# Hash bits of an attention head in three matmul passes instead of four

## The chip, the cores and the metric

One core of one Trainium2 chip runs the program. The metric is device time in microseconds (us) from start to end of one execution; the median of the runs counts.

## The reference

LSH attention over 2 batches of 8 heads (768 positions, head size 64) is followed by two gated dense blocks. Of the attention, what matters here:

```python
q_bits = (np.einsum('bhsd,dk->bhsk', q, proj) > 0)      # proj: 64 x 6
k_bits = (np.einsum('bhsd,dk->bhsk', k, proj) > 0)
q_bucket = np.sum(q_bits * 2 ** np.arange(6), axis=-1)  # same for k
mask = q_bucket[:, :, :, None] == k_bucket[:, :, None, :]
scores = np.where(mask, scale * q @ k.T, -1e9)
out = softmax(scores) @ v
```

Two positions attend to each other only if the signs of all six projections agree. A wrong sign changes a whole row, so the projection has to be close to exact.

## The kernel before, in words

The program works through 16 heads. For each, `prep` (L378) brings q and k into the form of matmul operands, six tiles of 128 queries then run through scores, maximum, exponential, transposition and the product with v, and the weights of the dense blocks are decoded from 64-bit numbers in between. The dense blocks follow; part of the first one runs beside the later heads.

Numbers are carried as two parts that a matmul takes at full speed, a high part (the number rounded) and a low part (what is left). `split` (L360) makes them with q and k apart, as 64 + 64 columns of a tile `spq` or `spk`. In `prep`, six transposes of such a tile go to `psT` buffers, tiles of PSUM of which there are four for the whole stage (`psT`, L278), and ScalarE copies them into `aq` or `ak` (L390): rows 0 to 63 hold the high part, rows 64 to 127 the low part. SyncE copies rows into `bq` and `bk` (L393, L395), the operands of the second score matmul.

The hash follows at L398 to L405. For each half of 384 positions one PSUM tile `gps` collects the projections of q in one set of rows and of k in the other:

```python
for n, nm in enumerate(("aq", "ak")):
    for x in range(2):
        pe.matmul(ps[:, :HS], lhsT=pq[n][x], rhs=m[nm][:, hs], start=n + x == 0, stop=n + x == 2)
```

`pq[n][0]` is the high part of the projection, `pq[n][1]` the low part, each placed for both the high and the low rows of the operand. VectorE turns signs into numbers (`ft`, L402), and SyncE copies them into the lower halves of the score operands (L406, L407). These numbers make the score of a pair with differing bits too small to matter. So `gps` is computed with four matmuls for each half, eight for a head, 120 for heads 1 to 15. Head 0 has its own code, `first_head`, with eight more (L447).

The order of the work is a list schedule: `order_engines` (L40) gives each instruction a cost and each hand-over between engines a delay, walks through time by priorities, and fixes the order of the rows on every engine, SyncE's queue included. An instruction that isn't ready holds up all that stands behind it on its engine. `prep` for the next head is spread over the tiles of the head before.

Of the kernel before, what the change touches and what calls it, by code (L numbers as in the profile page):

```python
# [11 lines left out]
F32R = mybir.dt.float32r  # L12
# [216 lines left out]
def lsh_attention_moe_moe2_kernel(  # L229
# [21 lines left out]
    B, H, S, D = q.shape  # L251
    P = 128
    NB = proj.shape[1]
    NT = S // P
    HS = S // 2
# [14 lines left out]
    dve = nc.vector  # L270
    pool = nc.gpsimd
    pe = nc.tensor
    sync = nc.sync
# [4 lines left out]
    def f(ap):  # L278
        return ap.bitcast(F32)

    cst = Tiles(ctx.enter_context(tc.tile_pool(name="cst", bufs=1, side="left")), "cst", 1)
# [6 lines left out]
    idr = cst.tile([P, P], F32R, name="idr")  # L288
    pq_raw = cst.tile([P, NB], F32, name="pq_raw")
    pq = [[cst.tile([P, P], F32R, name=f"pq{a}{i}") for i in range(2)] for a in "qk"]  # L290
    thr = cst.tile([P, 2], F32, name="thr")
    lim = cst.tile([P, 2], F32, name="lim")

# [56 lines left out]
    def load_head(h, nms):  # L350
        if not 0 <= h < NH:
            return
        b, hh = divmod(h, H)
        for nm, src in (("q", q), ("k", k), ("v", v)):
            if nm in nms:
                t = ap_.tile([P, NT, D], F32, tag="raw" + nm, name=f"raw{nm}{h}", bufs=1)
                sync.dma_start(out=t, in_=src[b, hh].rearrange("(p c) d -> p c d", c=NT))
                raws[h, nm] = t

    def split(h, nm, part):  # L360
        if not 0 <= h < NH:
            return
        if part == 0:
            t = ap_.tile([P, NT, 2, D], F32R, tag="sp" + nm, name=f"sp{nm}{h}", bufs=2 if nm == "v" else 1)
            splits[h, nm] = t
            (pool if h >= 2 else dve).tensor_copy(t[:, :, 0, :], raws[h, nm])
        else:
            t = splits[h, nm]
            (dve if h < 2 and nm != "v" else pool).tensor_tensor(out=t[:, :, 1, :], in0=raws[h, nm], in1=f(t[:, :, 0, :]), op=ALU.subtract)

    def alloc_mats(h):
        m = {}
        for nm in ("aq", "bq", "ak", "bk"):
            m[nm] = ap_.tile([P, S], F32R, tag=nm, name=f"{nm}{h}")
        m["ft"] = ap_.tile([P, S], F32R, tag="ft", name=f"ft{h}", bufs=1)
        mats[h] = m

    def prep(h):  # L378

        load_head(h, "v")  # L380
        if h < NH:
            alloc_mats(h)
            m = mats[h]
            for nm, d in (("q", "aq"), ("k", "ak")):
                t = splits[h, nm]
                for half in range(2):
                    ps = psT.tile([P, 512], F32R, tag="t", name="trr")
                    for c in range(3):
                        pe.transpose(ps[:, c * P:(c + 1) * P], t[:, half * 3 + c].rearrange("p a d -> p (a d)"), idr)
                    act.activation(out=m[d][:, half * HS:(half + 1) * HS], in_=f(ps[:, :HS]), func=AF.Copy,  # L390
                                   scale=SCALE if nm == "q" else 1.0)
                    if nm == "q" and half == 1:
                        sync.dma_start(out=f(m["bq"][0:D]), in_=f(m["aq"][0:D]))  # L393
                    yield
            sync.dma_start(out=f(m["bk"][0:D]), in_=f(m["ak"][D:P]))  # L395
            for half in range(2):
                hs = slice(half * HS, (half + 1) * HS)
                ps = psT.tile([P, 512], F32, tag="t", name="gps")  # L398
                for n, nm in enumerate(("aq", "ak")):
                    for x in range(2):  # L400
                        pe.matmul(ps[:, :HS], lhsT=pq[n][x], rhs=m[nm][:, hs], start=n + x == 0, stop=n + x == 2)  # L401
                dve.tensor_scalar(out=m["ft"][:, hs], in0=ps[:, :HS], scalar1=thr[:, 0:1], scalar2=thr[:, 1:2],  # L402
                                  op0=ALU.is_gt, op1=ALU.mult)
                if half == 0:
                    yield  # L405
            sync.dma_start(out=f(m["bk"][D:P]), in_=f(m["ft"][0:D]))  # L406
            sync.dma_start(out=f(m["bq"][D:P]), in_=f(m["ft"][D:P]))  # L407
            sync.dma_start(out=f(m["ak"][D:P]), in_=f(m["ak"][0:D]))
            yield
        for nm in "qk":  # L410
            split(h + 1, nm, 0)
            split(h + 1, nm, 1)
        load_head(h + 2, "qk")
        split(h - 1, "v", 0)
        split(h - 1, "v", 1)
# [391 lines left out]
    for n, (r0, sg) in enumerate(((D, 1.0), (0, -1.0))):  # L807
        for x in range(2):
            dve.memset(f(pq[n][x]), 0.0)
        for b0, sgn in ((r0, sg), (r0 + o, -sg)):  # L810
            hi, lo = (t[:, b0:b0 + NB] for t in pq[n])
            dve.tensor_scalar(out=hi, in0=pq_raw, scalar1=sgn, scalar2=None, op0=ALU.mult)
            dve.scalar_tensor_tensor(out=lo, in0=pq_raw, scalar=sgn, in1=f(hi), op0=ALU.mult, op1=ALU.subtract)
    dve.memset(thr[D:P, 1:2], -BIG)
    dve.memset(thr[0:D, 1:2], 1.0)
    dve.memset(thr[:, 0:1], 0.0)
# [19 lines left out]
    for _ in prep(1):  # L836
        pass
    pgs = {}

    def emit_prep(s):  # L840
        if s + 2 >= NT:
            h, i = divmod(s + 2, NT)
            if i == 0:
                pgs[0] = prep(h + 1)
            prio(s, -300)
            for _ in range(PAT[i]):
                next(pgs[0], None)
            if i == NT - 1:
                for _ in pgs[0]:
                    pass  # L850
# [74 lines left out]
```

## Time and profile before

| what | us |
|---|---|
| median of 3 runs | 856.51 (855.91 to 858.85) |
| the profiled execution, its own time | 857.49 |
| its span, first to last instruction | 855.5 |
| PE busy (share of the span) | 805.7 (94%) |
| DVE busy | 592.3 (69%) |
| ACT busy | 525.2 (61%) |
| POOL busy | 283.5 (33%) |
| mean granted clock of TensorE, of full speed | 0.996 |

The page's shares are averages over stages. Up to about 387 us the heads run and PE and DVE are both busy nearly all the time; from some 570 us on only dense matmuls are left and DVE has little to do. Matmul records overlap in a pipeline, so their mean length (some 350 ns for 384 columns) is not the time that one more matmul costs; the pieces of the chain, which don't overlap, tell that. The line names `PE`, `PEld` (weight load), `DVE` (VectorE), `ACT` (ScalarE), `POOL` (GpSimd) and `SP` (SyncE, which issues all transfers) are those of the profile.

### The profile page before, as it was taken

Reading aid. Unit: us, or ns where it says so; the run is one execution under the profiler, and the core shown is the slowest. Engines: PE = TensorE matmul, PEld = TensorE weight load, DVE = VectorE, ACT = ScalarE, POOL = GpSimd, SP = SyncE. Lnnn points to the kernel's source line nnn. Section 1 sums busy time; section 2 is a strip of 40 time slices with the busy share of each in tenths; the row PEclk is TensorE's granted clock in tenths of the full one; section 3 lists DMA queues with packets and bytes.
Section 4 is the critical chain, followed back from the end, with each engine's and each line's share of the span. In section 5 each row is a group of like instructions: output and inputs, shape, how many; then the busy total and the mean of one; then the engine's idle time right before and its main releaser. Section 6 shows DMA issues by size and latency. Waiting matters only on the chain.

```text
span 855.5 us, 12210 instructions
## 1 busy us (share of the span) xinstructions
PE 805.7 (94%) x4272; PEld 681.2 (80%) x4272; DVE 592.3 (69%) x1059; ACT 525.2 (61%) x1024; POOL 283.5 (33%) x236
## 2 busy tenths in 40 slices
PE   4777999999979999999999999999999999999998
PEld 3656888889878889897788777778888888888886
DVE  5999999998889999999569999972222222222222
ACT  4778878887778988888347656663334433343331
POOL 1343323232325343227423342343333323333230
PEclk9999999999989999999999999999999999999999
DMA  7555555443334544323105433400000000010001
GB/s 223 150 172 173 147 135 128 123 105 99 84 110 104 161 112 124 81 59 109 49 10 172 162 124 128 144 1 1 1 0 26 26 1 0 1 50 1 0 1 49
DMA packets 44908, 71.54 MB, mean 84 GB/s; under 512 B 6128, under 2 KB 32752, under 8 KB 44848
## 3 DMA queue, kind: packets, MB, share of 16 engines
q1 hardware_dynamic: 44848, 70.78, 28.7%
q8 instruction: 33, 0.54, 0.3%
q14 instruction: 27, 0.22, 0.1%
HBM read 52.43 MB, written 3.19 MB: 65 GB/s over the span
## 4 chain that ended last, share of the span: by engine, by line
PE 56%; DVE 29%; ACT 7%; issue 5%; DMA 2%; SPq 0%; DVEq 0%; ACTq 0%
PE pa L698 12%; PE m L698 11%; PE pb L698 11%; DVE da L338 4%; DVE pt L524 4%; PE tp L520 3%; PE av L537 3%; DVE s L476 3%; PE p L698 3%; DVE da L336 3%; PE wacc L593 3%; PE s L466 2%; PE gps L401 2%; ACT e L487 2%; PE s L469 2%
## 5 line engine op out<-in xcount | busy, mean ns | idle before, releaser
L738 DVE TENSOR_TENSOR pb<-pb,a 128x512 f32<-128x512 f32 x52 | 36.1, 694 | 138.8 <-PE pb L698 134.8
L520 PE MATMUL tp<-idf,e 128*128 128x128 f32 x576 | 100.8, 275 | 3.0 <-DVE pt L524 1.5
L524 DVE TENSOR_TENSOR pt<-tp,pt 128x384 fp32r<-128x384 f32 x192 | 100.7, 547 | 3.4 <-ACT pt L523 2.2
L523 ACT ACTIVATE pt<-tp 128x384 fp32r<-128x384 f32 x192 | 89.8, 494 | 21.1 <-PE tp L520 19.9
L487 ACT ACTIVATE e<-s,sm 128x768 f32<-128x768 f32 x96 | 95.9, 1000 | 10.2 <-DVE sm L477 9.7
L698 PE MATMUL pa<-x,wah 128*128 128x512 f32 x320 | 99.9, 390 | 1.4 <-DVE x L681 1.4
L698 PE MATMUL pb<-x,wbh 128*128 128x512 f32 x320 | 98.7, 389 | 0.0
L692 POOL TENSOR_TENSOR wal<-xall,wah 128x512 fp32r<-128x512 f32 x36 | 48.3, 1341 | 148.8 <-ACT wah L276 132.1
L476 DVE TENSOR_REDUCE s<-s 128x1 f32<-128x768 f32 x96 | 91.5, 954 | 8.6 <-PE s L469 8.5
L520 PEld LDWEIGHTS tp<-idf,e 128*128 128x128 f32 x576 | 71.5, 141 | 15.2 <-DVE pt L524 3.0
L334 ACT ACTIVATE da<-st 128x512 f32<-128x512 f32 x76 | 51.2, 673 | 47.0 <-DVE w1r L343 21.5
L537 PE MATMUL av<-pt,spv 128*128 128x256 f32 x576 | 78.7, 287 | 0.6 <-DVE pt L524 0.5
L537 PEld LDWEIGHTS av<-pt,spv 128*128 128x128 f32 x576 | 72.1, 191 | 2.8 <-DVE pt L524 0.9
L466 PE MATMUL s<-ak,aq 128*128 128x384 f32 x192 | 63.1, 385 | 9.3 <-ACT e L487 7.3
L698 PEld LDWEIGHTS pa<-x,wah 128*128 128x128 f32 x320 | 60.1, 188 | 14.7 <-DVE x L681 2.2
L593 PE MATMUL wacc<-wo,t 128*128 128x512 f32 x192 | 68.5, 420 | 2.9 <-POOL wo L588 1.4
L698 PEld LDWEIGHTS pb<-x,wbh 128*128 128x128 f32 x320 | 60.1, 188 | 12.5
L338 DVE SCALAR_TENSOR_TENSOR da<-st,da 128x512 uint32<-128x512 uint32 x76 | 64.6, 850 | 0.4
L698 PE MATMUL pa<-x,wal 128*128 128x512 f32 x160 | 62.3, 389 | 0.0
L698 PE MATMUL pb<-x,wbl 128*128 128x512 f32 x160 | 62.2, 389 | 0.0
L469 PE MATMUL s<-bk,bq 128*128 128x384 f32 x192 | 57.6, 365 | 0.0
L276 ACT ACTIVATE wah<-xall 128x512 fp32r<-128x512 f32 x36 | 22.7, 631 | 56.6 <-PE pa L698 56.6
(159 smaller groups left out, 1910.2 us busy)
## 6 DMA issues: line engine op xcount, KB each, us to landing
st<-in_moe_w_dram SPq DMA_DIRECT2D x32, 512.0 KB, 3.9
st<-in_moe_w_out_dram SPq DMA_DIRECT2D x20, 512.0 KB, 3.3
st<-in_moe_w_gate_dram SPq DMA_DIRECT2D x12, 512.0 KB, 3.5
st<-in_moe_w_val_dram SPq DMA_DIRECT2D x12, 512.0 KB, 3.5
rawq<-in_q_dram SPq DMA_DIRECT2D x16, 192.0 KB, 2.5
rawk<-in_k_dram SPq DMA_DIRECT2D x16, 192.0 KB, 3.3
rawv<-in_v_dram SPq DMA_DIRECT2D x16, 192.0 KB, 2.4
bq<-aq SPq DMA_DIRECT2D x16, 192.0 KB, 2.6
```

Source lines behind the costliest of these rows:

```text
L334: act.activation(out=f(a), in_=f(hw), func=AF.Abs)
L338: dve.scalar_tensor_tensor(out=a, in0=hw, scalar=0xC0000000, in1=a, op0=ALU.bitwise_and, op1=ALU.bitwise_or)
L466: pe.matmul(s[:, half, :HS], lhsT=m["aq"][:, qs], rhs=m["ak"][:, ks], start=True, stop=False)
L469: pe.matmul(s[:, half, :HS], lhsT=m["bq"][:, qs], rhs=m["bk"][:, ks], start=False, stop=True)
L476: dve.tensor_reduce(out=one[:, 1:2], in_=s[:, :, :HS], op=ALU.max, axis=AX.XY, negate=True)
L487: act.activation(out=e.rearrange("p (a c) -> p a c", a=2), in_=s[:, :, :HS], func=AF.Exp, bias=sm[:, 1:2], scale=sm[:, 0:1], accum_out=su_ ...
L520: pe.transpose(ps[:, j * P:(j + 1) * P], e[:, c * P:(c + 1) * P], idf)
L523: act.activation(out=dh, in_=src, func=AF.Copy)
L524: dve.tensor_tensor(out=lo[:, g % 2, half * 3:half * 3 + 3], in0=src, in1=f(dh), op=ALU.subtract)
L537: pe.matmul(acc[:, :2 * P].rearrange("p (a t) -> p a t", a=2), lhsT=w, rhs=r[:, :, c], start=(c == 0 and i == 0), stop=(c == NT - 1 and i ...
L593: pe.matmul(acc, lhsT=t3[x][:, j], rhs=wo[y][:, j], start=(j == 0 and n == 0), stop=(j == NF1 - 1 and n == 2))
L698: mm = pe.matmul(ps, lhsT=lhs[x], rhs=rhs[y], start=start and n == 0, stop=stop and n == 2)
```

## The change

The low part of the projection is needed against the high rows of q and of k only. The change lays these two sets of rows above each other in one operand: rows 0 to 63 of `bq` hold the high rows of q already, and a new copy puts the high rows of k into rows 64 to 127, which are free until `ft` is written there. A new constant `pl` stacks the two low parts of the projection, and one matmul with it takes the place of two. The products of the low part with the low rows, which were included before, fall away.

```diff
--- before.py
+++ after.py
@@ -288,6 +288,7 @@
     idr = cst.tile([P, P], F32R, name="idr")
     pq_raw = cst.tile([P, NB], F32, name="pq_raw")
     pq = [[cst.tile([P, P], F32R, name=f"pq{a}{i}") for i in range(2)] for a in "qk"]
+    pl = cst.tile([P, P], F32R, name="pl")
     thr = cst.tile([P, 2], F32, name="thr")
     lim = cst.tile([P, 2], F32, name="lim")
 
@@ -392,13 +393,13 @@
                     if nm == "q" and half == 1:
                         sync.dma_start(out=f(m["bq"][0:D]), in_=f(m["aq"][0:D]))
                     yield
+            sync.dma_start(out=f(m["bq"][D:P]), in_=f(m["ak"][0:D]))
             sync.dma_start(out=f(m["bk"][0:D]), in_=f(m["ak"][D:P]))
             for half in range(2):
                 hs = slice(half * HS, (half + 1) * HS)
                 ps = psT.tile([P, 512], F32, tag="t", name="gps")
-                for n, nm in enumerate(("aq", "ak")):
-                    for x in range(2):
-                        pe.matmul(ps[:, :HS], lhsT=pq[n][x], rhs=m[nm][:, hs], start=n + x == 0, stop=n + x == 2)
+                for n, nm in enumerate(("aq", "ak", "bq")):
+                    pe.matmul(ps[:, :HS], lhsT=pq[n][0] if n < 2 else pl, rhs=m[nm][:, hs], start=n == 0, stop=n == 2)
                 dve.tensor_scalar(out=m["ft"][:, hs], in0=ps[:, :HS], scalar1=thr[:, 0:1], scalar2=thr[:, 1:2],
                                   op0=ALU.is_gt, op1=ALU.mult)
                 if half == 0:
@@ -811,6 +812,8 @@
             hi, lo = (t[:, b0:b0 + NB] for t in pq[n])
             dve.tensor_scalar(out=hi, in0=pq_raw, scalar1=sgn, scalar2=None, op0=ALU.mult)
             dve.scalar_tensor_tensor(out=lo, in0=pq_raw, scalar=sgn, in1=f(hi), op0=ALU.mult, op1=ALU.subtract)
+    for n in range(2):
+        (act_copy if n else dve.tensor_copy)(pl[n * D:(n + 1) * D], f(pq[n][1][n * D:(n + 1) * D]))
     dve.memset(thr[D:P, 1:2], -BIG)
     dve.memset(thr[0:D, 1:2], 1.0)
     dve.memset(thr[:, 0:1], 0.0)
```

The new order was built with the same planner, and the rows of all engines moved. Three places are shown. First PE at the hash of head 11, `gps` with the preceding row, before (names end in the number of a tile, `aq_3212` and `ak_3214` are head 11's; line numbers are those of the file in question, one higher here after the change):

```order
L698 MATMUL p_3180<-xh,wl 128x512
L401 MATMUL gps<-aq_3212,pqq_72 128x384
L401 MATMUL gps<-aq_3212,pqq_73 128x384
L401 MATMUL gps<-ak_3214,pqk_74 128x384
L401 MATMUL gps<-ak_3214,pqk_75 128x384
L401 MATMUL gps<-aq_3212,pqq_72 128x384
L401 MATMUL gps<-aq_3212,pqq_73 128x384
L401 MATMUL gps<-ak_3214,pqk_74 128x384
L401 MATMUL gps<-ak_3214,pqk_75 128x384
L466 MATMUL s_83<-ak_2903,aq_2901 128x384 x2
L469 MATMUL s_83<-bk_2904,bq_2902 128x384 x2
```

and after the change, where `aq_3205`, `ak_3207` and `bq_3206` are head 11's:

```order
L521 MATMUL tp_3305<-idf,e_3183 128x128 x3
L402 MATMUL gps<-aq_3205,pqq_72 128x384
L402 MATMUL gps<-ak_3207,pqk_74 128x384
L402 MATMUL gps<-aq_3205,pqq_72 128x384
L402 MATMUL gps<-ak_3207,pqk_74 128x384
L699 MATMUL p_3334<-xh,wh 128x512
L521 MATMUL tp_3346<-idf,e_3224 128x128 x2
L402 MATMUL gps<-bq_3206,pl 128x384 x2
L467 MATMUL s_84<-ak_2897,aq_2895 128x384 x2
```

Two matmuls are gone, and the third pass of both halves stands behind the first two passes of both halves and three more matmuls, one of a dense layer (`p`) and two transposes (`tp`).

Second, PE at the hash of head 6, after the change, from right behind the second pass of the second half to the third passes:

```order
L467 MATMUL s_84<-ak_1370,aq_1368 128x384
L594 MATMUL wacc_1575<-wo_93,t_3_1499 128x512
L467 MATMUL s_84<-ak_1370,aq_1368 128x384
L594 MATMUL wacc_1575<-wo_92,t_3_1500 128x512
L470 MATMUL s_84<-bk_1371,bq_1369 128x384
L594 MATMUL wacc_1575<-wo_92,t_3_1499 128x512
L470 MATMUL s_84<-bk_1371,bq_1369 128x384
L594 MATMUL wacc_1575<-wo_93,t_3_1499 128x512
L594 MATMUL wacc_1575<-wo_92,t_3_1500 128x512
L578 MATMUL w3t_1808<-idf,w3f 128x128
L467 MATMUL s_85<-ak_1370,aq_1368 128x384
L402 MATMUL gps<-bq_1675,pl 128x384 x2
```

More rows of other work (`s` scores, `wacc` a product of weights, `w3t` its transposes) stand between the passes here than in head 11. Before, the four passes of each half were one block in this head too.

Third, SP's queue at the preparation of head 11, before:

```order
L393 DMA bq_3213<-aq_3212 64x768
L357 DMA rawq_3472<-in_q_dram 128x384
L395 DMA bk_3215<-ak_3214 64x768
L501 DMA row_3236<-rs_3233 128x6
L357 DMA rawk_3474<-in_k_dram 128x384
L408 DMA ak_3214<-ak_3214 64x768
L406 DMA bk_3215<-ft_3216 64x768
L407 DMA bq_3213<-ft_3216 64x768
```

and after the change:

```order
L394 DMA bq_3206<-aq_3205 64x768
L358 DMA rawq_3464<-in_q_dram 128x384
L502 DMA row_3229<-rs_3226 128x6
L396 DMA bq_3206<-ak_3207 64x768
L397 DMA bk_3208<-ak_3207 64x768
L506 DMA rr_2922<-row_3229 64x768
L358 DMA rawk_3466<-in_k_dram 128x384
L409 DMA ak_3207<-ak_3207 64x768
L319 DMA st<-in_moe_w_dram 128x4x128
L407 DMA bk_3208<-ft_3209 64x768
L408 DMA bq_3206<-ft_3209 64x768
```

The new copy `bq_3206<-ak_3207` comes right before the copy into `bk`, and the later copies are one row further back; the row copies (`row`, `rr`) moved as well.

## Rows read from the trace of the kernel before

**Rows 1.** Busy time of each engine by stage, whole run; columns in the first row.
```profile
core 0: us, PE busy (x) PEld busy (x) DVE busy (x) ACT busy (x) POOL busy (x), PEclk, DMA share, GB/s
0.00:20.00 20.00, 8.10 (x34) 7.25 (x35) 10.89 (x40) 9.04 (x17) 1.91 (x8) 1.00 0.79 229
20.00:387.00 367.00, 339.92 (x2232) 299.36 (x2231) 342.41 (x675) 297.25 (x626) 121.87 (x116) 0.99 0.45 122
387.00:570.00 183.00, 175.96 (x771) 142.02 (x770) 164.98 (x240) 112.85 (x204) 74.47 (x47) 1.00 0.32 104
570.00:855.50 285.50, 281.70 (x1242) 232.59 (x1240) 74.05 (x108) 106.09 (x180) 85.23 (x66) 1.00 0.03 12
```

**Rows 2.** The same view, the first 40 us of the heads.
```profile
20.00:60.00 40.00, 30.95 (x183) 24.96 (x181) 37.82 (x73) 30.17 (x62) 16.62 (x16) 1.00 0.55 159
```

**Rows 3.** Chain of waits from 20 to 387 us, shares by engine, tile and line.
```profile
by line: DVE pt L524 8.4%; PE tp L520 8.1%; PE av L537 7.6%; DVE s L476 7.0%; PE wacc L593 6.4%; PE s L466 5.3%; PE gps L401 5.2%; ACT e L487 5.0%; PE s L469 4.7%; issue 4.4%; PE p L698 3.9%; DVE da L338 3.1%; ACT pt L523 2.9%; DVE da L336 
```

**Rows 4.** Pieces of the chain: start us, length us, what, how many instructions.
```profile
221.99 0.47 PE wacc L593 x2
...
320.63 1.42 PE av L537 x12
...
322.79 0.35 PE s L469 x2
...
326.30 1.39 PE gps L401 x8
...
330.75 0.33 PE tp L520 x3
```

**Rows 5.** Timeline of head 15's preparation: start us, length us, engine, line, what.
```profile
343.16 0.46 PE L389 MATMUL trr<-idr,spk 128*128 128x128 f32 x3
...
344.63 0.47 SPq L395 DMA_DIRECT2D bk<-ak  x1
...
346.22 0.51 PE L401 MATMUL gps<-aq,pqq 128*128 128x384 f32 x2
...
347.31 0.67 DVE L402 TENSOR_SCALAR ft<-gps,thr 128x384 fp32r<-128x384 f32 x1
```

**Rows 6.** Instructions of line 408, which copies `ak[0:64]` up: min/median/max.
```profile
L408 SPq DMA_DIRECT2D ak<-ak x15: 461/467/549, 26.0 to 348.1; - x15
...
DMA to landing us min/median/max: 2.5/2.6/6.0
```

**Rows 7.** The same view for line 395, the copy into `bk` (ns, then us).
```profile
L395 SPq DMA_DIRECT2D bk<-ak x15: 461/467/468, 21.8 to 344.6; - x15
...
DMA to landing us min/median/max: 2.6/3.7/6.9
```

**Rows 8.** The start: timeline of DVE, then the chain's piece of the copy.
```profile
4.92 0.55 DVE L369 TENSOR_TENSOR spk<-rawk,spk 128x384 fp32r<-128x384 f32 x1
...
5.39 0.15 DVE L813 SCALAR_TENSOR_TENSOR pqk<-pq_raw,pqk 128x6 fp32r<-128x6 f32 x1
...
7.64 9.88 DMA ak<-ft
```

**Rows 9.** Waits of PE: who waited for whom, us in total, times, longest.
```profile
PE s L466 <- ACT e L487: 7.3, 5, 5.0
...
PE tp L520 <- DVE pt L524: 1.5, 2, 1.3
```

**Rows 10.** Busy time around 245 us (columns as in rows 1), and the chain's piece there.
```profile
240.00:245.00 5.00, 0.91 (x3) 0.91 (x4) 5.00 (x10) 3.11 (x6) 1.26 (x1) 0.72 0.38 131
245.00:250.00 5.00, 5.00 (x26) 4.87 (x25) 3.30 (x8) 1.87 (x5) 0.70 (x2) 0.59 0.08 28
...
246.59 2.56 PE av L537 x12
```

**Rows 11.** Costliest groups of the page: evictions of transposed halves, busy us, mean ns.
```profile
L524 DVE TENSOR_TENSOR pt<-tp,pt 128x384 fp32r<-128x384 f32 x192 | 100.7, 547 | 3.4 <-ACT pt L523 2.2
L523 ACT ACTIVATE pt<-tp 128x384 fp32r<-128x384 f32 x192 | 89.8, 494 | 21.1 <-PE tp L520 19.9
```

## Prediction

> **What bounds the kernel now.** I read the busy time by stage first [rows 1]: from 387 us on the program holds only dense layers, which the change does not touch. The reader should look at the stage from 20 to 387 us, where all 120 hash matmuls that change lie: PE is busy for 339.92 us of 367 and DVE for 342.41. Neither engine is far ahead of the other. PE's busy time is also generous, since matmul records overlap. At the spacing of back-to-back work on the chain [rows 4] (a transpose 0.33 / 3 = 0.11 us, a score matmul 0.35 / 2 = 0.175, one of `av` 1.42 / 12 = 0.118, a 512-column one 0.47 / 2 = 0.235, a hash matmul 1.39 / 8 = 0.174), the stage's 2,232 PE instructions need about 319 us. PE work therefore takes 367 / 319 = 1.15 of its bare length.
>
> The chain of waits, cut to this stage, goes back and forth between the two engines and gives `gps` 5.2% of it [rows 3], 19.1 us, of 120 x 0.174 = 20.9 us in all: nine tenths of the hash matmuls lie on the path that sets the end. Blocks of eight are unbroken PE work [rows 4].
>
> **The change, part by part.** *Removed:* one of four passes, two matmuls for each of 15 heads, so 30 x 0.174 = 5.22 us of PE. The bounds of the gain are 0, if DVE (342.41 of 367 us busy) simply becomes what is late, and 5.2, if all of it comes off the end. I take the chain's share, 0.91 x 5.22 = 4.8 us. It is nearest because the rows of the chain are those that set the end; DVE's work is not late next at most of these blocks, since the chain runs through PE there.
>
> *Added, a wait on the path:* the third pass reads `bq[64:128]`, which a new copy fills from `ak[0:64]`. Before, nothing stood between the copy of `ak` out of PSUM and `gps`. Now SP issues a transfer and PE waits for it if the rows in between don't cover it. In the head shown [rows 5] the transposes of k end at 343.62 (343.16 + 0.46) and SP issues at 344.63, 1.0 us later; I take 1.1 with the semaphore. The landing has two near rows. The copy of the same rows of `ak` to the same upper partitions took 2.6 us in the median [rows 6]. The copy issued where the new one now stands, right behind the loads, took 3.7, and 6.9 at the worst [rows 7]. So PE needs 3.7 us of other work from the end of the k transposes to the third pass, by the first row, and 4.8 by the second. I take 2.6, because source, size and target partitions are the same.
>
> What covers it is read from the new order at the spacings above, times 1.15: 2.2, 3.3, 4.6, 4.1, 6.1, 6.3, 5.6, 5.1, 4.1, 3.5, 2.9, 4.6, 4.0, 4.2 and 5.0 us for heads 1 to 15. At 3.7, heads 1, 2, 10 and 11 fall short, by 1.5, 0.4, 0.2 and 0.8. The first two lie before 60 us, where PE is busy only 30.95 of 40 us [rows 2], and I cost them at nothing; if that cover is gone they cost 1.9. That leaves 1.0 us; with some scatter of the landing I take 1.5. At 4.8 the shortfalls sum to 10.5, of which 6.4 lie behind head 2. The term's bounds are 0 and 10.5.
>
> *A rule on such copies.* The Trainium skill (DMA: Bandwidth & Descriptors, section Anatomy of one DMA — SWDGE (gpsimd) path) fits a copy as about 2.0 us fixed plus its bytes at 436 GB/s, an estimate of 2.45 us for 196,608 bytes, wherever it stands; the trace's 3.7 and 6.9 [rows 7] disagree, and these copies are issued by SP, not by GpSimd. By that rule the waits behind head 2 would be about 0.8 us and the time 0.7 lower than my sum; by [rows 7] the time is the first rival's.
>
> *The queues.* Every head adds one issue on SP, 0.467 us [rows 7], ahead of `bk<-ak` and of whatever follows; 15 of them are 7 us over 330, and the pushed copies are wanted only when that head's scores begin, which in the new order stand 8 to 14 us of PE work (at the spacings above) behind its third pass. I cost it at nothing. The later write of `bq[64:128]` with `ft` must wait for the third pass, but `ft` is made from that pass, so this adds no new wait. DVE's `ft` moves behind the third pass; what is queued behind it on DVE are evictions and decode steps, and if PE is late there, DVE is late too: the second rival.
>
> *The start.* Two copies build `pl`. The new order puts DVE's copy and one small operation ahead of the second half of the split of k, on the chain that leads to the transposes and the 9.88 us copy [rows 8]. Its price lies between 0.15 us, that small operation, and 0.55 us, the split itself, which handles more [rows 8]; for the two of them I take 0.3 us.
>
> **Sum.** -4.8 + 1.5 + 0.3 = -3.0 us against the profiled execution's own 857.49 us, so 854.5. That execution stood 0.98 above the median of 856.51, so in medians 853.5. A measurement can tell about 0.3%, 2.6 us, from no change; 853.5 is just outside.
>
> **The rivals.**
> *The landing eats the gain.* The copy lands as [rows 7] do, since in most heads a load of weights or of q stands directly ahead of it on SP. Then 6.4 us of waits take the place of 1.5: 853.5 + 4.9 = 858.4 if all of it counts, 856 if half is covered by DVE work that PE would have waited for anyway. For it: same place in the queue. Against: the larger cover of heads 3 to 9.
>
> *Slower: the hash tiles hold two of the four `psT` buffers.* Before, a tile's first matmul and the start of its `ft` are 347.31 - 346.22 = 1.1 us apart [rows 5]. Now both tiles are opened by their first two passes and stay open until the copy has landed, 2 to 4 us in most heads, while transposes and `av` share the other two. A transposed half holds its buffer for 0.33 + 0.494 + 0.547 = 1.4 us [rows 4, 11]. If one such half per head waits for one eviction by DVE, 15 x 0.547 = 8.2 us come on top: 861.7. Against it: PE waited only 1.5 us for these evictions in the whole run [rows 9]. It decides for slower from 5.7 us of such waits on.
>
> *The clock falls.* PE's one wait of 5.0 us for `e` [rows 9] was followed by a granted clock of 0.72 and 0.59 of 2.4 GHz, on average between the two levels [rows 10], and an `av` group took 2.56 instead of 1.42 us. If a copy lands at 6.9, PE waits 1.1 + 6.9 - 3 = 5 us, and such a stop costs about 7: 860.5. The Trainium skill (TensorE: Matmul & The Clock Gate, section HAM oscillation — how this bites in real kernels) shows a kernel whose waits for transfers throttle every tile; by that, each late head would pay. The shorter waits that I expect are against it.
>
> *The old stall goes.* The order around 240 us changes too. If the 5.0 us wait and the slow clock behind it vanish, about 7 us more are saved: 846.5. The rows of DVE work that caused it stand there in nearly the same sequence, which speaks against it.
>
> **Chances.** Forecast 0.42 (its own range 851 to 855.5), landing rival 0.27 (855 to 859), buffers 0.18 (858 to 863), clock 0.05, stall gone 0.08. Of the forecast about 0.32 lies below 853.9, with the 0.08 this gives 0.40 for faster. Within 0.3% are the other 0.10 of the forecast and 0.22 of the landing rival, 0.32. Slower: 0.05 of the landing rival, 0.18 and 0.05, so 0.28. The range from 848 to 862 leaves out most of the vanished stall and the upper end of the buffers and the clock, under 0.2.
>
> **What would show it.** Right: 90 hash matmuls in place of 120 and the new copy landing at 2.5 to 3 us; PE's waits for DMA `bq<-ak` a few us in total, in heads 1, 2, 10 and 11; the stage of the heads shorter by about 3 us, the dense stage unchanged at 285 us. Wrong: landings near 3.7 with waits in most heads; waits of `tp` for `pt` well above 1.5 us; DVE waiting for `gps` for more than a few us; a second dip of the granted clock.

## The result, and the profile after

The changed kernel takes 867.57 us in the median (866.35 to 868.77, 4 runs) beside 857.00 for the kernel before (855.91 to 858.85, 4 runs): ratio 1.0118 (1.0103 to 1.0133), some 10 us slower where 3 us faster was forecast. Below, ratios are turned into time at 857.0 us. Their intervals are 1.0 to 2.4 us to either side, and a difference of two such times is uncertain by some 1.7 us. The profiled execution after took 868.77 us with a span of 867.0.

Busy time by stage after, the same events as borders (columns as in [rows 1]):

```profile
20.00:394.00 374.00, 341.39 (x2195) 296.76 (x2194) 340.69 (x677) 298.46 (x630) 124.21 (x117) 0.97 0.48 128
394.00:581.00 187.00, 178.47 (x774) 144.37 (x774) 161.99 (x237) 111.83 (x201) 73.94 (x47) 0.98 0.31 100
581.00:867.00 286.00, 282.11 (x1244) 232.92 (x1242) 74.46 (x108) 106.46 (x180) 85.28 (x66) 1.00 0.03 12
```

Against [rows 1] the heads are 7 us longer, the stage behind them 4, and the dense stage is the same. So there are two places to look at. PE's waits name both:

```profile
PE s L467 <- ACT e L488: 7.9, 5, 4.4
PE gps L402 <- DMA bq<-ak: 6.9, 6, 2.9
...
PE y L699 <- DVE gl L659: 5.0, 1, 5.0
...
PE tp L521 <- DVE pt L525: 1.7, 5, 0.5
```

`bq<-ak` is the new copy, and this wait is new. The view of the tile `bq` gives 12.2 us for it. That counts a matmul and the weight load in front of it apart, though they mostly stand idle at the same time; with the longer of the two at each stop it is 9.2 us in nine heads. The line of the copy, 396, gives its landing:

```profile
L402 PE MATMUL gps<-bq,pl x30: 331/338/448, 24.9 to 356.7; 128*128 128x384 f32 x30
...
  DMA bq<-ak: 12.2, 12
```

```profile
L396 SPq DMA_DIRECT2D bq<-ak x15: 467/467/1144, 21.4 to 352.6; - x15
...
DMA to landing us min/median/max: 2.7/3.4/7.2
```

The worst is head 5, in the timeline (start us, length us, engine, line, what, in brackets the wait ahead of it):

```profile
120.48 0.33 SPq L319 DMA_DIRECT2D st<-in_moe_w_dram  x1
...
120.90 0.47 SPq L396 DMA_DIRECT2D bq<-ak  x1
...
122.83 0.33 PE L402 MATMUL gps<-ak,pqk 128*128 128x384 f32 x1
...
128.27 0.59 PE L402 MATMUL gps<-bq,pl 128*128 128x384 f32 x2 [2.85 <-DMA bq<-ak]
...
128.72 1.26 DVE L403 TENSOR_SCALAR ft<-gps,thr 128x384 fp32r<-128x384 f32 x2 [2.58 <-PE gps L402]
```

A load of weights, `st`, of 512 KB was issued 0.42 us ahead on the same queue. In this kernel the landing of each copy follows how far ahead such a load stands:

| head | `st` issued ahead by, us | copy lands after, us |
|---|---|---|
| 5 | 0.42 | 7.2 |
| 6 | 0.48 | 5.8 |
| 7 | 0.71 | 5.4 |
| 3 | 1.04 | 3.9 |
| 12 | 1.16 | 4.3 |
| 14 | 1.57 | 3.2 |
| 2 | 1.87 | 2.7 |
| 4 | 2.65 | 2.7 |

In the other seven heads, with no `st` within 2.6 us ahead, it lands after 2.7 to 3.5 us.

The second place is the start of the dense work. There VectorE makes `gl`, the low part of an operand (`p` less its high part `gh`), and the dense matmul `y` reads it. PE waits 5.0 us for `gl`, idles from 415 us on, and then works at half clock, 1.2 GHz (windows of 5 us, columns as in [rows 1]):

```profile
415.00:420.00 5.00, 0.81 (x4) 0.35 (x2) 5.00 (x6) 0.41 (x1) 2.83 (x2) 1.00 0.35 105
420.00:425.00 5.00, 4.16 (x10) 3.29 (x11) 4.46 (x8) 0.34 (x1) 0.00 (x0) 0.50 0.36 108
425.00:430.00 5.00, 5.00 (x20) 4.05 (x19) 0.69 (x1) 1.68 (x4) 2.62 (x3) 0.82 0.00 0
```

### The profile page after: what moved, and what is told of

It is laid out like the page before. It is cut to its first block, busy times and chain, and to the rows that moved or that the text cites. A ratio compares the mean times of both kernels' runs of the same rounds, so it can differ in the third digit from the quotient of the medians.

```text
span 867.0 us, 12169 instructions
## 1 busy us (share of the span) xinstructions
PE 810.4 (93%) x4242; PEld 681.5 (79%) x4242; DVE 587.8 (68%) x1060; ACT 525.0 (61%) x1025; POOL 285.2 (33%) x236
## 4 chain that ended last, share of the span: by engine, by line
PE 57%; DVE 25%; ACT 6%; DMA 5%; issue 5%; POOL 1%; SPq 0%; DVEq 0%; ACTq 0%; POOLq 0%
PE pa L699 12%; PE m L699 11%; PE pb L699 11%; PE av L538 5%; PE tp L521 4%; DVE da L339 4%; DMA bq<-ak 4%; PE wacc L594 3%; DVE da L338 3%; DVE da L337 3%; PE p L699 3%; DVE s L477 3%; PE s L467 2%; DVE pt L525 2%; PE s L470 2%
## 5 line engine op out<-in xcount | busy, mean ns | idle before, releaser
L521 PE MATMUL tp<-idf,e 128*128 128x128 f32 x576 | 103.7, 279 | 3.5 <-DVE pt L525 1.7
L594 PE MATMUL wacc<-wo,t 128*128 128x512 f32 x192 | 70.5, 429 | 6.5 <-ACT wo L276 5.3
L470 PE MATMUL s<-bk,bq 128*128 128x384 f32 x192 | 60.8, 373 | 0.0
```

The costliest lines, as they stand in the source:

```text
L470: pe.matmul(s[:, half, :HS], lhsT=m["bq"][:, qs], rhs=m["bk"][:, ks], start=False, stop=True)
L521: pe.transpose(ps[:, j * P:(j + 1) * P], e[:, c * P:(c + 1) * P], idf)
L594: pe.matmul(acc, lhsT=t3[x][:, j], rhs=wo[y][:, j], start=(j == 0 and n == 0), stop=(j == NF1 - 1 and n == 2))
```

## The experiments

Theory A: the third pass waits for the copy. Rivals: B, any new order of the planner costs this; C, the hash tiles hold `psT` buffers. Diffs are against the changed kernel unless said otherwise.

**1. The wait taken away.** The third pass reads `aq` in place of the copy, which is still issued. The planner is told that it reads `bq`, so that the order of all engines stays as it was.

```diff
-                for n, nm in enumerate(("aq", "ak", "bq")):
+                for n, nm in enumerate(("aq", "ak", "aq")):
```

> The changed kernel with the same order of rows on every engine and the new copy still issued, but the third pass reads aq in place of bq, so nothing waits for the copy (the low part of the projection of k is left out, that of q taken with the wrong rows as well). Theory A, the wait for the copy is the loss: the time falls to 853 to 858 us, PE's waits for DMA bq<-ak (6.9 us before it) vanish, and so do the dips of the granted clock in heads 3 to 6. Theory B, the new order of the rows is itself the loss: 865 to 868 us, as with the wait. Theory C, the two PSUM tiles held until the copy lands: as theory A for the time, but PE's waits of gps for the eviction pt (3.5 us) stay.

Measured: 857.88 us, ratio 1.0002 (0.9987 to 1.0018). The wait alone is worth 9.9 us, in the very same order, so the order isn't to blame for it. The sign that was set for C is there, `gps` still waits 3.5 us for `pt`; but it waited 3.5 us with the copy's wait too, and `tp` waits 1.7 us for `pt` in both, so these buffers hold no visible part of the 9.9. Still, this kernel has 30 matmuls less than before and no price for the copy, and gains nothing. Its last exponential starts at 376.9 us (before 380.9), its first `m` of the dense stage at 567.6 (before 568.3): in these two executions what the heads gain is lost at

```profile
PE y L711 <- DVE gl L671: 5.1, 1, 5.1
```

In the kernel before, the same row of this stretch (393 to 440 us) reads

```profile
PE y L698 <- DVE gl L658: 1.6, 1, 1.6
```

Times within one profiled execution scatter: the kernel before and experiment 8 have the same order up to 404 us, and their last exponentials start at 380.9 and 384.1. So the 4.0 us of the heads are a rough figure.

**2. The copy by GpSimd**, in place of the transfer, with its own order:

```diff
-            sync.dma_start(out=f(m["bq"][D:P]), in_=f(m["ak"][0:D]))
+            pool.tensor_copy(m["bq"][D:P], f(m["ak"][0:D]))
```

> The changed kernel with the copy of ak[0:64] into bq[64:128] made by GpSimd (one copy of 64x768 for each head) in place of a transfer; the planner makes another order. Theory A: GpSimd's copy takes about 1 us against a median landing of 3.4 and up to 7.2, the waits mostly vanish, and the time is 851 to 857 us. Theory B: the order is a third one, with nothing that favours it, 855 to 868 us.

Measured: 865.3 us, ratio 1.0090 (1.0066 to 1.0114). GpSimd makes the copy in 0.82 us, and no row of PE waits for it:

```profile
L396 POOL CAST bq<-ak x15: 817/824/1503, 21.8 to 346.0; 64x768 fp32r<-64x768 f32 x15
```

Yet the time is nearly that of the changed kernel. The wait of `y` for `gl` stays at 5.0 us and `s` waits 12.7 us for `e` (7.9 after the change). Two things changed at once, the copy and the order, so this tells only that rival B is possible in another order: an order without the wait can be as slow.

**3. The wait alone, in the old order.** The kernel before, with four passes; the last of them now reads `bq` behind the same copy, and the planner's order is kept. (`n + x == 2` holds for the fourth pass alone; the recorded expectations of 3 and 4 call it the third.)

```diff
+            cp = sync.dma_start(out=f(m["bq"][D:P]), in_=f(m["ak"][0:D]))
...
-                        pe.matmul(ps[:, :HS], lhsT=pq[n][x], rhs=m[nm][:, hs], start=n + x == 0, stop=n + x == 2)
+                        mm = pe.matmul(ps[:, :HS], lhsT=pq[n][x], rhs=m["bq" if n + x == 2 else nm][:, hs], start=n + x == 0, stop=n + x == 2)
```

> The kernel before with its order and its four passes, but the third of them reads bq[0:128], after the same new copy from ak, in place of ak, so that the wait is there and the order is the old one; the planner is not told of the copy (the third product is that of other rows). Theory A: the old order leaves only about 1 to 3 us between the end of the k transposes and this pass, a copy takes 1.1 + 3.4 us, so PE stands 1.5 to 3.5 us in each of 15 heads: 875 to 900 us. Theory B: the wait costs little, 857 to 862 us.

Measured: 900.71 us, ratio 1.0509 (1.0481 to 1.0537), with these waits of `gps` for the copy:

```profile
PE gps L417 <- DMA bq<-ak: 32.1, 14, 6.4
```

With the weight loads, the longer of the two at each stop, it is 34.7 us. The time grew by 44 us, so a wait on this path shows in full, and more. The granted clock was 0.94 from 20 to 430 us (0.99 in [rows 1]), which may hold the rest; no run separates it.

**4. The gain alone, in the old order.** The kernel before, its last pass only 8 of 384 columns wide:

```diff
-                        pe.matmul(ps[:, :HS], lhsT=pq[n][x], rhs=m[nm][:, hs], start=n + x == 0, stop=n + x == 2)
+                        w = 8 if n + x == 2 else HS
+                        mm = pe.matmul(ps[:, :w], lhsT=pq[n][x], rhs=m[nm][:, half * HS:half * HS + w], start=n + x == 0, stop=n + x == 2)
```

> The kernel before with its order, where the third of four passes takes 8 columns in place of 384 (its product is left out for the others), so PE work is removed and no wait is added. If PE's saved time comes off the end as the share of gps on the chain said: 30 matmuls save some 4 us, 852 to 854 us, by theories A and B alike. If DVE keeps the end: 856 to 857 us.

Measured: 856.12 us, ratio 0.9989 (0.9975 to 1.0003). A narrow matmul isn't free, since it still has its weight load and a record of 167 ns:

```profile
L413 PE MATMUL gps<-ak,pqk x60: 167/250/421, 21.4 to 347.8; 128*128 128x384 f32 x30, 128*128 128x8 f32 x30
```

From head 3 on the blocks of `gps` are 3.5 us shorter in sum, 0.13 us for each narrow matmul. So about 4 us of PE's work are gone, not the whole 5.2, and the time falls by 0.9 us, give or take 1.2. That is far from the share of 0.91 that the prediction took. In the two profiled executions the last exponential starts at 381.0 us, and at 380.9 before: no sign of shorter heads.

**5. More work ahead of the third pass.** The planner reckons the copy 3 us later.

```diff
-                        done = dma + 900
+                        done = dma + 900 + (3000 if ins[k].name in Tiles.slow else 0)
```

> The changed kernel; the planner alone is told that the new copy lands 3 us later than it reckoned, so it puts more of TensorE's other work between the copy and the third pass (by the planner's own widths 2.7 to 6.1 us a head, where the changed kernel has 1.5 to 4.6). Theory A (the third pass waits for the copy, and too little work stands before it): the waits for bq fall from 6.9 us to under 1.5 us and the time to about that of the run without the wait, 857.9 us, so 856 to 860. Rival B (any new order of the planner costs this much, the wait or not): 864 to 868 stays. Rival C (the hash tiles, open for longer now, hold two of the four psT buffers and stop the transposes): the waits for bq go, but tp waits for pt grow by 5 us or more, and the time is over 864. In the stretch from 393 to 440 us all of them leave the loss of about 4 us at y, which waits 5 us for gl.

Measured: 865.52 us, ratio 1.0097 (1.0080 to 1.0113). The waits for `bq` are nearly gone (0.6 us), and the time stays, as rivals B and C said. Idle time ahead of the transposes of `e`, by what ended it (matmuls and weight loads added up, so one stop can count twice):

```profile
  DVE pt L528: 11.3, 19
  DVE ft L406: 7.4, 6
```

Before, the same rows read

```profile
  DVE pt L524: 4.4, 7
...
  DVE ft L402: 0.9, 2
```

and after the change 5.9 and 1.0 us. Ahead of `av`, `ft` ends another 7.4 us (0.2 before, 1.4 after the change). PE's own wait of `tp` for `pt` grew from 1.7 to 4.5 us, less than the 5 that was set as C's sign. These rows speak for C even so: the hash tiles are open for longer, and their buffers are missed. That this is the cause is argued from them; the run meant to confirm it, 9, did not.

**6. The copy on ScalarE's own queue.**

```diff
-            sync.dma_start(out=f(m["bq"][D:P]), in_=f(m["ak"][0:D]))
+            act.dma_start(out=f(m["bq"][D:P]), in_=f(m["ak"][0:D]))
```

> The changed kernel with only the issue of the new copy moved from SP's queue to ScalarE's own queue. If the copy is late because it stands behind the loads of the weights (st, 524 kB) and of the heads on SP's queue, its landing falls from 3.4 us in the middle and 7.2 us at worst to about 2.6 us with little spread, the waits for bq fall from 6.9 us to under 2 us, and the time is 858 to 861. If it is late because all queues share the same 16 DMA engines, which the loads fill, the landing keeps its worst cases of 5 us and more, the waits stay at 5 us or over, and the time stays at 864 to 868. If ScalarE pays for the issue (15 issues, in front of exp or of the eviction of ak), s waits for e grow by 2 us or more.

Measured: 890.12 us, ratio 1.0380 (1.0360 to 1.0401). Another queue doesn't get past the loads:

```profile
L400 ACTq DMA_DIRECT2D bq<-ak x15: 468/498/514, 20.5 to 375.4; - x15
...
DMA to landing us min/median/max: 3.6/4.3/7.1
```

It lands later in the middle (4.3 for 3.4), and `gps` waits 18.9 us for it. `s` waits 11.0 us for `e` (7.9 after the change), the sign set for ScalarE paying for the issue. The time is far above every range that was given. The order differs too, so the 20 us aren't split further. The Trainium skill (DMA: Bandwidth & Descriptors, section Issuing engines are not separate DMA queues) says that transfers of all engines interleave on the same DMA engines whoever issues them; the worst landing of 7.1 agrees.

**7 and 8. VectorE's order at the start of the dense work.** Experiment 7 is 5 with this edit, 8 is the kernel before with it:

```diff
+                        if fi == 5:
+                            late["gl"] = o.ins
...
+            with tc.issue_after(late["gl"]) if n < 3 else nullcontext():
-            for _ in range(decodes(n)):
-                decode()
+                for _ in range(decodes(n)):
+                    decode()
...
+                with tc.issue_after(late["gl"]):
-                split_x(2, x2[2], range(KC))
+                    split_x(2, x2[2], range(KC))
```

> The run with more work before the third pass, and in addition VectorE's first decodes and the split of the third slice of x in the second part are queued behind the sixth gl of the first part. Theory: what the three passes gain in the heads, 3.7 us, is lost at one place, where y waits 5.0 us for gl behind five decode operations and three splits on VectorE, and TensorE then runs at half clock for some 7 us. Then the wait of y goes to under 0.5 us, the dip behind it goes too, and the time is 3.5 to 6 us below that of the same kernel without this edit: 851 to 856. Rival: TensorE is waiting there for the whole of VectorE's and GpSimd's work, so the same wait comes back at the next p, pa or pb, and the time is within 1 us of the same kernel without this edit.

> Control: the kernel before, with its four passes, and only the same edit of VectorE's order at the sixth gl. There y waits 1.6 us for gl and pa 1.4 us for x in the stretch from 393 to 440 us, and no dip of the clock follows. If the edit is worth only the wait that it takes away, 0.5 to 2 us: 855 to 857. If the new place of the decodes is worth more by itself, so that the run with three passes owes its gain to it and not to the passes, this one falls by 4 us or more too: 853 or less. The difference between this run and the run with three passes and the same edit is what the removed pass is worth once its copy is covered; by the terms of the prediction 4.8 us, by the run with the narrow third pass in the old order about 1 us.

Measured: 860.83 us, ratio 1.0041 (1.0027 to 1.0055), and for the kernel before 855.38, ratio 0.9973 (0.9961 to 0.9984). The wait of `y` for `gl` is gone in both (0.2 us left in 8). The edit is worth 4.8 us with three passes and 2.3 with four; 7 as a whole is above the 851 to 856 that was expected.

**9 and 10. The pass with the copy first.** Experiment 5 with the passes in another order, so that the tile is opened only when the copy is there; 10 adds VectorE's edit.

```diff
-                for n, nm in enumerate(("aq", "ak", "bq")):
+                for n, nm in ((2, "bq"), (0, "aq"), (1, "ak")):
```

> The run with the copy planned 3 us later, and the pass that reads the copy is put first of the three, so that the hash tile of psT is taken only once the copy is there and all three passes stand together. Theory C (with the copy covered, what costs is that the hash tile of psT is held from its first pass over the whole cover, so tp and av wait for ft to give a buffer back): tp and av idle before them until DVE ft fall from 7.4 us each to the 1 us of the kernel before, the waits for bq stay under 2 us, and the time falls from 865.5 to 856 to 860. Rival (any order that puts the hash later costs this, through scores that start later): the waits move to s, for ak<-ft and for e, and the time stays at 863 to 867.

> The same, with VectorE's decodes and the split of the third slice queued behind the sixth gl. That edit was worth 4.7 us beside the covered copy (865.5 to 860.8) and 1.7 us in the kernel before (857.1 to 855.4). If both effects are separate, this run is 4 to 5 us below the run without it: 852 to 856, at or below the kernel before with the same edit, 855.4. If the removed pass is worth its 4.8 us once nothing is paid for the copy: 851 or less. If VectorE and ScalarE hold the stage anyway: 855 to 857.

Measured: 882.79 us, ratio 1.0298 (1.0284 to 1.0312), and 880.71, ratio 1.0286 (1.0268 to 1.0304). Both expectations of theory C failed. `s` now waits 22.1 us for `e` (7.3 before, [rows 9]), and `tp` still stands idle 10.3 us until `ft`. VectorE's edit gives 1.0 us here, not 4 to 5. The hash came late for the scores, it seems: the last exponential starts at 404.1 us. Why `ft` still holds `tp` up wasn't followed further.

**11. No wait and VectorE's edit**, experiment 1 with the diff of 7:

> Leaves the dependence of the third pass on the copy out: it reads aq in place of the copy (the copy is still issued), in the changed kernel's order of all engines, plus the edit of VectorE's order at the sixth gl. An upper bound on what three passes can gain here: the run without the wait was 857.9 us and lost 5.0 us at y. If y's wait is what took the gain of the heads (3.7 us by the profile) away, 852.5 to 855. If the stretch is bound by VectorE's and GpSimd's work in any order, 856.5 to 858.5. Against the kernel before with the same edit (855.4) this run gives the worth of the removed passes with no price for the copy at all.

Measured: 853.46 us, ratio 0.9959 (0.9947 to 0.9972), 3.7 us below experiment 1. Against the kernel before with the same edit the three passes are worth 0.0014, 1.2 us, plus or minus 1.5 (the two half-widths, 0.00125 and 0.00115, taken in quadrature give 0.0017). The two kernels also differ in their order, so this is the worth of passes and order together.

**12 and 13. The copy in two halves**, the first right behind the first half of `ak`; the order of TensorE, VectorE, ScalarE and GpSimd is the changed kernel's, row for row. 13 adds VectorE's edit.

```diff
+                    if nm == "k" and half == 0:
+                        cp = sync.dma_start(out=f(m["bq"][D:P, 0:HS]), in_=f(m["ak"][0:D, 0:HS]))
...
-            sync.dma_start(out=f(m["bq"][D:P]), in_=f(m["ak"][0:D]))
+            cp = sync.dma_start(out=f(m["bq"][D:P, HS:S]), in_=f(m["ak"][0:D, HS:S]))
```

> The changed kernel with the new copy in two halves of 98 kB, the first issued after the first half of ak is evicted (0.5 to 1.7 us before the second), the second where the whole copy stood; the order of TensorE, VectorE, ScalarE and GpSimd is the changed kernel's, row for row. If the wait is for the copy's landing, the first half is there 0.5 to 1.7 us sooner and the second third pass comes 0.3 us or more behind the first, so the 12.2 us that the rows of the third pass stand idle for the copy fall to 4 to 8 us and the time from 867.6 to 861 to 864. If most of the landing is queueing behind the loads on SP's queue, both halves wait as long as the whole did, 15 more issues of 0.47 us delay what is behind them, and the time is 866 to 870.

> The same, with VectorE's decodes and the split of the third slice queued behind the sixth gl: y's wait of 5.0 us for gl goes, worth 4.4 us in the pair of runs without the wait for the copy (857.9 to 853.5). Expected 4 to 5 us below the run without it, so 856 to 860 if the half copies help, 862 to 866 if not. Below the kernel before with the same edit (855.4) only if the waits for the copy fall under 2 us.

Measured: 865.5 us, ratio 1.0096 (1.0080 to 1.0112), and 860.67, ratio 1.0038 (1.0022 to 1.0055). The time falls by 1.9 us, give or take 1.9, less than expected, and `gps` waits 7.9 us for the halves, not less than for the whole copies (6.9). The second halves, with half the bytes, land nearly as late as the whole copies did:

```profile
DMA to landing us min/median/max: 2.1/3.0/7.2
```

The 7.2 is head 5 again, where `st` was issued 0.50 us ahead. So the size of the copy isn't what makes the late ones late.

**14 and 15. The loads behind the copy.** One edit of SP's queue, in six heads (2, 3, 5, 6, 7 and 12): a load `st` that stands directly ahead of the copies is issued behind them. The other four engines' rows are the changed kernel's, one for one. 15 adds VectorE's edit.

```diff
+    q = order["SP"]
+    for n in range(len(q) - 2):
+        if [ins[q[n]].name in Tiles.loads] + [ins[k].name in Tiles.copies for k in q[n + 1:n + 3]] == [True] * 3:
+            q[n:n + 3] = q[n + 1:n + 3] + q[n:n + 1]
```

> The changed kernel with one edit of SP's queue: where a load of weights (st, 524 kB) stands directly ahead of the new copy, in six heads (2, 3, 5, 6, 7 and 12), it is issued behind the two copies instead; the rows of the other four engines are the changed kernel's, one for one. In the changed kernel the copy lands 7.2, 5.8 and 5.4 us after its issue in heads 5, 6 and 7, where the load stood 0.4 to 0.7 us ahead, 3.9 and 4.3 in heads 3 and 12 (1.0 and 1.2 us ahead), and 2.7 in heads whose load stood 1.9 us and more ahead. If the load directly ahead makes the copy late, the worst landing falls from 7.2 to under 4 us, the waits for bq from 6.9 to under 2 us, and the time from 867.6 to 858 to 861. If the copies are late for the DMA engines' load in general, whoever stands ahead, the landing keeps worst cases over 5 us and the time stays at 865 to 868. A price may show: decode waits for st, or tiles of rawk and ak land later.

> The same with VectorE's decodes and the split of the third slice queued behind the sixth gl, worth 4 to 5 us beside three passes so far. If the load ahead was the cause: 853.5 to 856.5, since the bound without any wait is 853.5; this would be at or below the kernel before with the same edit (855.4). If not: 860 to 864, as with the half copies (860.7).

Measured: 859.88 us, ratio 1.0032 (1.0019 to 1.0045), and 854.55, ratio 0.9973 (0.9961 to 0.9985). Landing of both copies (`bq` and `bk`) and the wait for `bq` in experiment 14:

```profile
DMA to landing us min/median/max: 2.7/3.0/4.7
```

```profile
PE gps L412 <- DMA bq<-ak: 2.8, 3, 1.2
```

The worst landing falls from 7.7 us (the `bk` copies after the change) to 4.7, and 7.4 us of time go by moving six transfers by two places. The time is in the expected range; a worst landing under 4 us and waits under 2 us were not quite reached. So the loads ahead made the copies late in this kernel.

How far ahead the load was issued isn't the whole of it, though. In experiment 5 two copies landed after 6.3 and 6.0 us with `st` 2.87 and 1.74 us ahead, and in 6, on the other queue, two after 7.1 and 6.2 us with it 1.88 and 1.77 us ahead. In all four that load itself had 2.9 to 5.0 us still to go when the copy was issued, and in heads 5, 6 and 7 of the changed kernel 4.9 to 5.6 us. In these three runs no copy took over 5.3 us without such a load under way, on whichever queue the copy was.

In 15 `y` waits no longer for `gl`, and the stretch that idled and ran at half clock before is full:

```profile
405.00:410.00 5.00, 5.00 (x23) 4.15 (x23) 5.00 (x4) 1.70 (x3) 4.89 (x4) 1.00 0.01 3
410.00:415.00 5.00, 4.52 (x20) 3.39 (x19) 5.00 (x7) 1.44 (x3) 3.92 (x3) 1.00 0.00 0
415.00:420.00 5.00, 3.84 (x17) 3.19 (x18) 2.90 (x5) 1.01 (x2) 0.30 (x1) 1.00 0.66 210
```

Experiment 15 keeps the change and beats the kernel before by 0.27%. So does the kernel before with VectorE's edit alone (8), by as much.

**The sum of it**, in us against the kernel before:

| kernel | by ratio |
|---|---|
| changed | +10.1 |
| changed, six loads behind the copy (14) | +2.7 |
| changed, no wait for the copy (1) | +0.2 |
| changed, no wait, VectorE's edit (11) | -3.5 |
| before, VectorE's edit (8) | -2.3 |

Read downwards: the loads directly ahead of the copy cost 7.4 us, the rest of the wait for it 2.5, VectorE's order at `gl` 3.7, and what the three passes leave over four is 1.2. The kernel before loses 2.3 at `gl` as well, so only 1.4 of the 3.7 came with the new order, and 9.9 + 1.4 - 1.2 gives the 10.1. The wait is clear of the noise; 1.4 and 1.2 are not.

## Why the prediction was wrong

**The wait, +1.5 in the sum, was 9.9.** The step that failed is "I take 2.6, because source, size and target partitions are the same". What is copied didn't decide the landing; the load still under way did. [Rows 7] had it, with 3.7 in the middle and 6.9 at the worst for a copy at this very place: in the trace before, the 6.9 is head 5's, with `st` issued 0.42 us ahead, and the next, 4.9, head 7's, with 0.48. The upper bound drawn from it, 10.5, is close to what was measured by luck, since its shortfalls lie in heads 1, 2, 10 and 11 above all. The second fault is one size for every head. At 3.7 us the prediction saw heads 1, 2, 10 and 11 fall short; of these, 1, 2 and 11 landed after 2.7. The longest waits fell in heads 5, 6 and 7 (2.85, 1.59 and 1.51 us), which it gave the most cover, 6.1, 6.3 and 5.6 us, and where the copy took 7.2, 5.8 and 5.4 us on top of the 1.1 us to its issue.

**The landing rival** was the right mechanism, reason included ("a load of weights or of q stands directly ahead of it"), but it held a median of the landing for the price and so came to 4.9 us over the forecast where the wait alone was 8.4 over its term. The delay isn't the same in each head, and the sum of waits is made by the worst landings.

**The gain, -4.8, was 0.9 in the old order, for about three quarters of the pass's work, and 1.2, give or take 1.5, in the new one.** The step was the chain's share of `gps`, 0.91 of its matmuls: it was taken as what a shorter PE would give. The prediction's own lower bound, "0, if DVE simply becomes what is late", is nearer. Experiment 4 shows it: some 4 us of PE less, and 0.9 less time. That DVE is what holds the rest was argued, from its 342 us of 367, and not tried. A chain tells what ended last, not what comes next once that is shorter. A smaller slip: at the spacings that it names, the stage's PE rows sum to 327 us and not 319, so the factor on the cover is 1.12 for 1.15; this changes nothing in the outcome.

**What the prediction didn't have:** VectorE's order at the start of the dense work. In the kernel before `y` waited 1.6 us for `gl`. In the new order PE comes to that place 27.5 us after the start of the last exponential (28.5 before), and `gl`, behind six decode operations and three splits (four and two before), starts 32.2 us after it (29.8 before). The wait is 5.0 us, with a dip of the clock behind it. In the run without the copy's wait:

```profile
404.49 0.39 PE L711 MATMUL y<-gh,wh 128*128 128x512 f32 x1
...
405.43 1.48 DVE L349 TENSOR_SCALAR da<-da 128x512 uint32<-128x512 uint32 x1
406.83 0.68 DVE L694 TENSOR_TENSOR x<-xall,x 128x512 fp32r<-128x512 f32 x1
...
409.24 0.68 DVE L671 TENSOR_TENSOR gl<-p,gh 128x512 fp32r<-128x512 f32 x1
...
409.97 0.79 PE L711 MATMUL y<-gl,wh 128*128 128x512 f32 x1 [5.09 <-DVE gl L671]
```

**The other rivals.** The hash tiles didn't hold up the transposes in the changed kernel (`tp` waits 1.7 us for `pt`, 1.5 in [rows 9]); once the cover was lengthened, the rows of 5 say that they did. The old stall around 240 us didn't go: `s` waits 7.9 us for `e` (7.3 in [rows 9]). The clock rival was right for one head: behind head 5's wait TensorE fell to half clock, 1.2 GHz, for part of the next 5 us (columns as in [rows 1]), and no such fall stands there in experiment 1:

```profile
125.00:130.00 5.00, 2.05 (x13) 1.27 (x11) 2.19 (x5) 1.45 (x4) 0.00 (x0) 0.99 0.95 202
130.00:135.00 5.00, 4.96 (x28) 4.90 (x28) 3.65 (x7) 3.60 (x9) 0.00 (x0) 0.67 0.53 132
```

What that fall cost is part of the 9.9 and isn't told apart. The dip behind `y` was longer (the rows with 0.50 and 0.82 in the section on the result). The mean clock was 0.984 after and 0.996 before, in the profiled executions, but 0.982 in experiment 15, which is faster than both, so the mean explains nothing here. The +0.3 at the start can't be told: the first exponential starts at 21.9 us after, 21.6 before, and at 21.4 and 20.7 in experiments 1 and 11 with the same start. The dense stage took the 287 us from first `m` to end that it took before.

## What to carry to other kernels

A transfer that a matmul waits for is priced by what is still under way when it is issued, head by head, not by the median of a like copy; look for a bulk load issued shortly ahead of it, and issue the bulk behind it. Another queue didn't help here. Before the gain of a shorter engine is taken from the chain, ask what the other engine does in the same stretch: with VectorE busy for 342 of 367 us, 5.2 us less of TensorE gave about 1. When a planner makes a new order, look also at places that the change doesn't touch, since the engines may come to them with other work queued ahead.

## What was not expected of the hardware

**VectorE beside GpSimd.** In the stretch before `gl` an operation of VectorE on SBUF can take nearly four times as long while GpSimd works on SBUF beside it. In the kernel before, within 7 us:

```profile
404.18 1.64 POOL L692 TENSOR_TENSOR wal<-w1r,wah 128x512 fp32r<-128x512 f32 x1
404.59 1.51 DVE L336 TENSOR_SCALAR da<-da 128x512 f32<-128x512 f32 x1
...
410.36 0.41 DVE L336 TENSOR_SCALAR da<-da 128x512 f32<-128x512 f32 x1
```

The same `da` takes 1.51 us beside GpSimd's 1.64, and 0.41 where GpSimd rests (from 409.3 to 414.3 us). Over the whole run, 45 of the 76 operations of L336 have no operation of GpSimd beside them, and none of these takes over 0.43 us; the other 31 take 0.76 us in the mean. The Trainium skill (SBUF — State Buffer, section Who interferes with whom) says that the two share a pair of ports under an exclusive lock, so that one waits for the other's whole instruction; the durations shown agree. The planner's cost for this `da` is 69 + 512 x 0.52 = 335 ns, whatever GpSimd does, so it will have reckoned the queue in front of `gl` as shorter than it was; no run tried it with another cost.

**Half the bytes, the same worst landing.** Behind a load of 512 KB a copy of 98 kB landed after 7.2 us at worst, as one of 197 kB did.
